# Soft-MoE attention kernel: four key chunks of 112, tokens transposed in 32x32 blocks on VectorE, slot sums in 16 array tiles

## The chip, the cores and the metric

The kernel runs on one core of a Trainium2 chip. A core has five engines that run side by side and wait for one another through semaphores: TensorE (PE in the profile, its weight loads PEld), VectorE (DVE), ScalarE (ACT), GpSimd (POOL) and SyncE (SP, which here only issues DMAs). Matrix products go from SBUF, the working memory, into PSUM, the memory of sums. The metric is the device time of one execution in microseconds, the median of several runs.

## What is computed

Eight batches of twelve heads, 448 tokens and 64 features per head. Attention uses a sigmoid in place of a softmax; its output, 3584 tokens of 768 features, goes through a soft mixture of experts with 32 slots (8 experts of 4).

```
scores = scale * q @ k.T - log(448);  attn = 1 / (1 + exp(-scores))
x = concat_heads(attn @ v)                          # (3584, 768)
logits = x @ phi                                    # (3584, 32)
d = softmax of logits over all tokens;  slot_input = d.T @ x      # (32, 768)
for e in range(8): slot_out[e] = relu(slot_input[e] @ w1[e]) @ w2[e]
c = softmax of logits over the 32 slots;  out = c @ slot_out      # (3584, 768)
```

All inputs are float32.

## The kernel before

**Attention.** The loop at L481 runs over 48 pairs of heads (six pairs `hp` to a batch `b`). A pair has the two heads' 64 features on the two halves of the 128 partitions. The 448 keys are cut into three chunks of 128 and a rest of 64. The rests of the two heads make one chunk of their own ("middle", step 0 of `qk_step` and `av_step`): a block-diagonal matrix of 128 x 128 with zeros beside each head's 64 keys, so that one product serves both heads. q and k are split into a high part rounded to fp32r and a low part, and a score is the sum of three fp32r products (high-high, high-low, low-high; L339 for the middle, L351 for the others, where the two heads' products lie on the two halves of the array's rows). ScalarE turns the scores into attention (`att`, L344 and L354). Attention times V (L375) is in plain fp32, two heads side by side in the array's columns; the middle chunk splits its attention and V too (L358, L144, L372). The sum `av` is copied to SBUF as `xT` (L381), 128 features by 448 tokens.

**Logits and slots.** `logits_job` (L183) adds a pair's part of the logits of a batch, four blocks of 112 tokens in four column groups of the array. `tr_job` (L193, L194) transposes `xT` on TensorE into `xtok`, token by feature. When a batch is complete, its softmax over tokens is carried along as a running maximum (`softmax_a` to `softmax_c`); `dt_job` transposes the weights on TensorE (L241), and `slot_job` forms weights times tokens (L251: eight products of 384 columns) and adds it to `acc`.

**Order.** All engines but POOL run in the order in which the program writes their instructions. For each pair the order is a string of tokens (L36 to L39): `Q1` to `Q3`, `V0` to `V3` are score and V steps, `P0` the next pair's middle scores, `L` and `T` the previous pair's logits and transposes, `k..`, `qp..`, `v..` the splits of the next pair, `l..` its loads. `EDGE`, `AFTER` and `THIRD` are the strings of a batch's first three pairs, in which the batch before is finished: its softmax in the first, its slot sums (`S0`, `S1`) in the second.

**Loads.** SP issues every DMA, in program order. Four tiles per pair (q with the middle keys, k, V, middle V) are loaded one or two pairs ahead, as the tiles come free. Beside them the expert weights are fetched in units of 384 KB (`load_unit`) into a ring: 55 tiles `wa` and two `kt` during attention, and twelve tiles `wb` whose space is that of the attention's tiles, and which can be loaded only as those are released, in order of address (the pools are opened as `ldq`, `ldr`, `sp`, `at`, `ldv`, `xp`). There are 128 units in all, so the other 59 follow as the experts free the ring.

**The rest.** `last_job` finishes the last batch; then the experts' first products (L517), the second ones (L630), and the output (`out_batch`), which writes 32 DMAs of 336 KB.

Of the kernel before, what the change touches and what calls it, by code (L numbers as in the profile page):

```python
# [26 lines left out]
N_A = 55  # L27
N_B = 12
QW = S + P
KW = 3 * P  # L30
# [5 lines left out]
ORDER = "n lq e mhV k00V k01 Q1 lw ml L T k10V Q2 k11 Q3 V0 qp0V qp1 lQ V1 V2 V3 P0 lv v0 v1 lr"  # L36
THIRD = "n lq e mhV k00V k01 sc Q1 ml L T k10V Q2 k11 lw Q3 V0 qp0V qp1 lQ V1 V2 V3 P0 v0 v1 lv lr"
EDGE = "e n k00V mhV k01 Q1 lq ml L sa T k10V Q2 k11 Q3 sb lw V0 qp0V qp1 lQ V1 V2 V3 P0 lv v0 sr v1 lr"
AFTER = "n mhV k00 eA Q1 dt lq ml k01 Q2 S0 k10V S1 k11 L lw T Q3 V0 qp0V qp1 lQ V1 V2 v0V V3 P0 v1 lr lv"  # L39
# [4 lines left out]
def soft_moe_attention(ctx: ExitStack, tc: tile.TileContext, qk, v, phi, w1, w2, cst, out):  # L44
# [6 lines left out]
    ldk = ctx.enter_context(tc.tile_pool(name="ldk", bufs=2))  # L51
# [8 lines left out]
    lt_all = cpool.tile([CH, NLT, P], F32, name="lt_all")  # L60
# [12 lines left out]
    def ring_tile(dt=F32):  # L73
        n = state["ring"]
        state["ring"] = n + 1
        n %= N_A + 2 + N_B
        if n < N_A:
            return wpa.tile([P, UNIT], dt, name=f"wa{n}")
        if n < N_A + 2:
            return ldk.tile([P, UNIT], dt, name="kt")  # L80
        return state["wpb"].tile([P, UNIT], dt, name=f"wb{n - N_A - 2}")

# [10 lines left out]
    lo, hi = slice(0, 64), slice(64, 128)  # L93
# [3 lines left out]
    lg_all = ps_lg.tile([P, 512], F32, name="lg")[:, 0:NLT * CH].rearrange("p (b t) -> p b t", b=NLT)  # L97

    with ExitStack() as actx:
        ldq = actx.enter_context(tc.tile_pool(name="ldq", bufs=1))  # L100
        ldr = actx.enter_context(tc.tile_pool(name="ldr", bufs=1))
        sp = actx.enter_context(tc.tile_pool(name="sp", bufs=1))
        at = [actx.enter_context(tc.tile_pool(name=f"at{i}", bufs=1)) for i in range(4)]
        ldv = actx.enter_context(tc.tile_pool(name="ldv", bufs=1))
# [5 lines left out]
        kts = {}  # L110
        qts = {}
        vts = {}
        vms = {}
        splits = {}
        xams = {}

        def load_k(p):
            kt = ldk.tile([P, UNIT], F32, name="kt")
            nc.sync.dma_start(kt[:, 0:KW], qk[p][:, QW:])
            kts[p] = kt  # L120

        def load_q(p):
            qt = ldq.tile([P, QW], F32, name="qt")
            nc.sync.dma_start(qt[:], qk[p][:, 0:QW])
            qts[p] = qt

        def load_v(p):
            vt = ldv.tile([P, NCH - 1, P], F32, name="vt")
            nc.sync.dma_start(vt[:], v[p][:, 1:, :])
            vts[p] = vt  # L130

        def load_vm(p):
            vm = ldr.tile([P, P], F32, name="vr")
            nc.sync.dma_start(vm[:], v[p][:, 0, :])
            vms[p] = vm

        def split_tiles(p):
            ks = [sp.tile([P, 2, P], F32R, name="ks0"), sp.tile([P, 2, KW], F32R, name="ks1", bufs=2)]
            qs = sp.tile([P, 2, S], F32R, name="qs")
            vm = sp.tile([P, 2, P], F32R, name="vm")  # L140
            splits[p] = (qs, ks, vm)

        def low_part(dst, src):
            nc.vector.tensor_tensor(out=dst[:, 1, :], in0=src, in1=dst[:, 0, :].bitcast(F32), op=ALU.subtract)  # L144

        def q_part(p, z, copy):
            qs = splits[p][0]
            if z == 0:
                copy(qs[:, 0, :], qts[p][:, 0:S])  # L149
            else:  # L150
                low_part(qs, qts[p][:, 0:S])

        def k_part(p, i, z, copy=nc.vector.tensor_copy):
            ks = splits[p][1][i]
            src = qts[p][:, S:] if i == 0 else kts[p][:, 0:KW]
            if z == 0:
                copy(ks[:, 0, :], src)
            else:
                nc.vector.tensor_tensor(out=ks[:, 1, :], in0=src, in1=ks[:, 0, :].bitcast(F32), op=ALU.subtract)  # L159

        def v_part(p, z, copy=nc.vector.tensor_copy):
            vm, src = splits[p][2], vms[p][:]
            if z == 0:
                copy(vm[:, 0, :], src)
            else:
                nc.vector.tensor_tensor(out=vm[:, 1, :], in0=src, in1=vm[:, 0, :].bitcast(F32), op=ALU.subtract)

        xtok = {}
        lgp = {}
        dts = {}  # L170
        av = {}
        xTs = {}
        atts = {}
        ams = {}

        def logits_job(p):
            b, hp = divmod(p, NPR)
            xT = xTs[p]
            if hp == 0:
                lgp[b] = lg_all[:, b % NLT, :]  # L180
                xtok[b] = xp.tile([CH, NCH, DM], F32, name="xtok")
            for j in reversed(range(NCH)):
                nc.tensor.matmul(  # L183
                    lgp[b][32 * j:32 * j + 32, :], phi_sb[:, hp, :], xT[:, j * CH:(j + 1) * CH],
                    start=(hp == 0), stop=(hp == NPR - 1),
                )

        def tr_job(p):
            b, hp = divmod(p, NPR)
            xT = xTs[p]  # L190
            pt = ps_ms.tile([P, NCH, P], F32, name="ms")
            for j in range(NCH):
                nc.tensor.transpose(out=pt[0:CH, j, :], in_=xT[:, j * CH:(j + 1) * CH], identity=ident)  # L193
            nc.scalar.copy(xtok[b][:, :, hp * P:(hp + 1) * P], pt[0:CH, :, :])  # L194

        def softmax_a(b):
            t1 = small.tile([P, 2, P], F32, name="t1")
            t2 = small.tile([P, 2, P], F32, name="t2")
            ls, zt = t2[:, 0, 0:CH], t1[:, 0, :]
            if b < NLT:  # L200
                nc.scalar.copy(ls, lgp[b])
            else:
                ls = lgp[b]
            if b == 0:
                nc.vector.tensor_reduce(out=mz[:, 0:1], in_=ls, axis=AX.X, op=ALU.max)
            else:
                m1 = small.tile([P, 2], F32, name="m1")
                nc.vector.tensor_reduce(out=m1[:, 0:1], in_=ls, axis=AX.X, op=ALU.max)
                nc.vector.tensor_copy(m1[:, 1:2], mz[:, 0:1])
                nc.vector.tensor_tensor(out=mz[:, 0:1], in0=m1[:, 0:1], in1=m1[:, 1:2], op=ALU.max)  # L210
                nc.vector.tensor_tensor(out=zt[:, CH:CH + 1], in0=m1[:, 1:2], in1=mz[:, 0:1], op=ALU.subtract)
            nc.vector.tensor_scalar(zt[:, 0:CH], ls, mz[:, 0:1], None, op0=ALU.subtract)
            dts[b] = (t1, t2)

        def softmax_b(b):
            t1, t2 = dts[b]
            zt, pe = t1[:, 0, :], t1[:, 1, :]
            n = CH if b == 0 else CH + 1
# [3 lines left out]
        def softmax_r(b):  # L222
            zt, pe = dts[b][0][:, 0, :], dts[b][0][:, 1, :]
            n = CH if b == 0 else CH + 1
# [3 lines left out]
        def softmax_c(b):  # L228
            pe = dts[b][0][:, 1, :]
            if b == 0:  # L230
                nc.vector.tensor_reduce(out=mz[:, 1:2], in_=pe[:, 0:CH], axis=AX.X, op=ALU.add)
            else:
                zb = small.tile([P, 1], F32, name="zb")
                nc.vector.tensor_reduce(out=zb[:], in_=pe[:, 0:CH], axis=AX.X, op=ALU.add)
                nc.vector.scalar_tensor_tensor(
                    out=mz[:, 1:2], in0=mz[:, 1:2], scalar=pe[:, CH:CH + 1], in1=zb[:], op0=ALU.mult, op1=ALU.add)

        def dt_job(b):
            t1, t2 = dts[b]
            pt = ps_ms.tile([P, NCH, P], F32, name="ms")  # L240
            nc.tensor.transpose(out=pt[0:CH, 1, :], in_=t1[:, 1, 0:CH], identity=ident)  # L241
            if b < NLT:
                nc.tensor.transpose(out=pt[0:CH, 0, :], in_=t2[:, 0, 0:CH], identity=ident)
            nc.vector.tensor_copy(t2[0:CH, 1, :], pt[0:CH, 1, :])
            if b < NLT:
                nc.scalar.copy(lt_all[:, b, :], pt[0:CH, 0, :])

        def slot_mm(b, hf, pt, dT):
            cs = slice(hf * HALF, (hf + 1) * HALF)
            for j in reversed(range(NCH)):  # L250
                nc.tensor.matmul(  # L251
                    pt[32 * j:32 * j + 32, 0:HALF], dT[:, 32 * j:32 * j + 32], xtok[b][:, j, cs],
                    start=True, stop=True)

        def slot_job(b, hf):
            pe, dT = dts[b][0][:, 1, :], dts[b][1][0:CH, 1, :]
            pt = ps_ms.tile([P, 512], F32, name="ms")
            cs = slice(hf * HALF, (hf + 1) * HALF)
            slot_mm(b, hf, pt, dT)
            if b == 0:  # L260
                nc.vector.tensor_copy(acc[:, cs], pt[:, 0:HALF])
            else:
# [431 lines left out]
```

## Time and profile before

| | us |
|---|---|
| median of 3 runs (466.55 to 466.9) | 466.64 |
| the profiled execution's own time | 465.93 |
| its span, first to last instruction | 464.1 |
| TensorE busy | 439.0 |
| VectorE busy | 267.4 |
| ScalarE busy | 235.5 |
| mean granted TensorE clock | 0.981 |

The span is what the profile explains; 1.83 us of the profiled execution's time lie outside it. A busy TensorE is not one at its peak: products are pipelined, and how far a step has moved is seen from the starts of one block and of the next, not from the busy time.

### The profile page before, as it was taken

What the parts mean: (1) busy time and instruction counts of PE and PEld (TensorE: products, weight loads), DVE (VectorE), ACT (ScalarE), POOL (GpSimd) and SP (SyncE); (2) the same over time, 40 slices, a digit from 0 to 9 for tenths busy, and PEclk for the clock granted to TensorE, in tenths of its full rate; (3) what the DMA queues carried; (4) which work ended last, traced back from release to release, by engine and by line L of the source; (5) the groups of instructions that cost most, each with busy time, mean ns of one, the idle gap of its engine ahead of it and who ended that gap; (6) DMA issues with size and microseconds to landing.
All of it is one profiled execution on the core that took longest, in us unless ns stands there. A gap on an engine that the chain in (4) does not pass through costs nothing.

```text
span 464.1 us, 8634 instructions
## 1 busy us (share of the span) xinstructions
PE 439.0 (95%) x3270; PEld 232.9 (50%) x3270; DVE 267.4 (58%) x735; ACT 235.5 (51%) x363; POOL 2.4 (1%) x12
## 2 busy tenths in 40 slices
PE   8999999999999999999999999999999999879870
PEld 5555555555545455454545555554545555334340
DVE  5656665576657565765666575666654544535280
ACT  4546554564646465555646455565547111544260
POOL 0000000000000000000000000000000100000000
PEclk9999999999999999999999999999999999998985
DMA  5666555665656566465755656633335999999998
GB/s 184 162 196 202 155 184 151 203 173 153 213 147 191 135 200 194 139 195 162 208 165 167 184 158 191 189 109 109 90 105 185 337 399 400 401 401 400 389 288 260
DMA packets 54089, 98.31 MB, mean 212 GB/s; under 512 B 5664, under 2 KB 31520, under 8 KB 54048
## 3 DMA queue, kind: packets, MB, share of 16 engines
q1 hardware_dynamic: 54048, 97.77, 65.6%
q8 instruction: 25, 0.41, 0.4%
q14 instruction: 16, 0.13, 0.1%
HBM read 86.74 MB, written 11.01 MB: 211 GB/s over the span
## 4 chain that ended last, share of the span: by engine, by line
PE 88%; DVE 4%; issue 2%; ACT 2%; DMA 1%; DVEq 0%; ACTq 0%
PE av L375 25%; PE sc L351 23%; PE av L372 8%; PE sc L339 8%; PE ms L193 6%; PE lg L183 3%; PE ph L517 3%; PE ms L251 2%; PE po L630 2%; PE ph L605 1%; PE pt L534 1%; PE pt L605 1%; PE av L392 1%; DMA out_dram<-wa 1%; DVE tmp L530 1%
## 5 line engine op out<-in xcount | busy, mean ns | idle before, releaser
L354 ACT ACTIVATE att<-sc,nbias 128x896 f32<-128x896 f32 x144 | 140.6, 1009 | 15.6 <-PE sc L351 10.1
L375 PE MATMUL av<-att,vt 128*64 128x448 f32 x576 | 118.8, 548 | 0.0
L351 PE MATMUL sc<-qs,ks 64*128 64x448 f32 x864 | 115.6, 387 | 0.3 <-ACT att L354 0.3
L344 ACT ACTIVATE att<-sc,nbias 128x448 f32<-128x448 f32 x48 | 30.5, 635 | 131.9 <-PE sc L339 131.9
L351 PEld LDWEIGHTS sc<-qs,ks 64*128 64x128 f32 x864 | 73.0, 184 | 28.1 <-issue 22.1
L381 DVE COPY att<-av 128x448 f32<-128x448 f32 x41 | 25.6, 625 | 72.9 <-PE av L375 72.9
L375 PEld LDWEIGHTS av<-att,vt 128*64 128x64 f32 x576 | 37.1, 136 | 59.2 <-issue 55.9
L358 DVE CAST ah<-att 128x448 fp32r<-128x448 f32 x48 | 18.9, 394 | 40.9 <-ACT att L344 40.9
L372 PE MATMUL av<-ah,vm 128*128 128x448 f32 x144 | 42.3, 401 | 0.0
L339 PE MATMUL sc<-qs,ks 128*128 128x448 f32 x144 | 41.9, 399 | 0.0
L339 PEld LDWEIGHTS sc<-qs,ks 128*128 128x128 f32 x144 | 23.6, 190 | 33.8 <-issue 27.5
L194 ACT COPY xtok<-ms 112x512 f32<-112x512 f32 x48 | 28.2, 587 | 10.3 <-PE ms L193 10.3
L372 PEld LDWEIGHTS av<-ah,vm 128*128 128x128 f32 x144 | 23.3, 188 | 15.9 <-DVE ks L159 7.8
L193 PE MATMUL ms<-csb,att 128*112 128x128 f32 x192 | 31.1, 285 | 0.0
L144 DVE TENSOR_TENSOR qs<-qt,qs 128x448 fp32r<-128x448 f32 x48 | 30.0, 626 | 1.6
L144 DVE TENSOR_TENSOR ah<-att,ah 128x448 fp32r<-128x448 f32 x48 | 29.7, 618 | 0.0
L159 DVE TENSOR_TENSOR ks<-kt,ks 128x384 fp32r<-128x384 f32 x48 | 26.8, 557 | 1.4
L149 DVE CAST qs<-qt 128x448 fp32r<-128x448 f32 x48 | 18.8, 392 | 8.9 <-PE sc L351 6.4
L193 PEld LDWEIGHTS ms<-csb,att 128*112 128x112 f32 x192 | 19.4, 133 | 8.2 <-issue 7.0
L183 PE MATMUL lg<-att,phit 128*32 128x112 f32 x384 | 19.0, 269 | 0.8 <-DVE att L381 0.8
L517 PE MATMUL ph<-wa,sT 128*32 128x256 f32 x330 | 19.6, 381 | 0.0
L609 DVE COPY wa<-pt 112x384 f32<-112x384 f32 x28 | 14.4, 554 | 5.1 <-PE pt L605 4.9
(142 smaller groups left out, 329.0 us busy)
## 6 DMA issues: line engine op xcount, KB each, us to landing
wa<-in_w_dram SPq DMA_DIRECT2D x110, 384.0 KB, 6.0
qt<-in_qk_dram SPq DMA_DIRECT2D x48, 288.0 KB, 2.8
out_dram<-wa SPq DMA_DIRECT2D x28, 336.0 KB, 4.9
kt<-in_qk_dram SPq DMA_DIRECT2D x48, 192.0 KB, 3.6
vt<-in_v_dram SPq DMA_DIRECT2D x48, 192.0 KB, 2.4
wb<-in_w_dram SPq DMA_DIRECT2D x14, 384.0 KB, 5.4
vr<-in_v_dram SPq DMA_DIRECT2D x48, 64.0 KB, 2.2
kt<-in_w_dram SPq DMA_DIRECT2D x4, 384.0 KB, 5.8
```

Source lines behind the costliest of these rows:

```text
L144: nc.vector.tensor_tensor(out=dst[:, 1, :], in0=src, in1=dst[:, 0, :].bitcast(F32), op=ALU.subtract)
L159: nc.vector.tensor_tensor(out=ks[:, 1, :], in0=src, in1=ks[:, 0, :].bitcast(F32), op=ALU.subtract)
L183: nc.tensor.matmul(lgp[b][32 * j:32 * j + 32, :], phi_sb[:, hp, :], xT[:, j * CH:(j + 1) * CH], start=(hp == 0), stop=(hp == NPR - 1),)
L193: nc.tensor.transpose(out=pt[0:CH, j, :], in_=xT[:, j * CH:(j + 1) * CH], identity=ident)
L194: nc.scalar.copy(xtok[b][:, :, hp * P:(hp + 1) * P], pt[0:CH, :, :])
L339: nc.tensor.matmul(sc[:, 0, 0:S], ks[0][:, z, :], qs[:, y, :], start=(z + y == 0), stop=(z == 1))
L344: nc.scalar.activation(am, sc[:, 0, 0:S], AF.Sigmoid, bias=nbias[:], scale=QSCALE)
L351: nc.tensor.matmul(sc[:, r.start // 64, 0:S], ks[1][r, z, (s - 1) * P:s * P], qs[r, y, :], start=(z + y == 0), stop=(z == 1))
L354: nc.scalar.activation(att[:], sc[:, :, 0:S], AF.Sigmoid, bias=nbias[:], scale=QSCALE)
L372: nc.tensor.matmul(av[p][:, 0:S], vm[:, z, :], att[:, y, :], start=(z + y == 0), stop=False)
L375: nc.tensor.matmul(av[p][64 * h:64 * h + 64, 0:S], vt[:, s - 1, 64 * h:64 * h + 64], att[:, h, :], start=False, stop=(s == 3))
L517: nc.tensor.matmul(ph[32 * j:32 * j + 32, uu, :], sT[:, 3 * kh + kc, :], utile[("w1", e, 2 * uu + j // 2, kh)][:, kc * 256:(kc + 1) * 256] ...
```

## The change

**Key chunks.** The keys are cut into four chunks of 112, all alike. The middle chunk, its splits and its zeros go. `split` makes the high and low parts of q and k with four VectorE instructions of 448 columns. q and k of a pair come in one DMA (448 KB), V in one (224 KB), the first into a single buffer, the second into two.

**Order.** The token strings go. One pair is: the previous pair's copy of `av`, all four score steps, the previous pair's logits, all four V steps, the splits of the next pair, the loads of the pair after that. The scores have three PSUM buffers in place of two.

**Tokens.** `tr_job` goes. VectorE transposes `xT` in blocks of 32 x 32 (`turn`), so a block of 32 tokens lies on each group of 32 partitions, with features in 32s. The order of the query tokens is permuted on the host so that the logits' blocks fit.

**Slots.** The softmax weights `pe` of a batch are transposed in the same way into `z`, and `spread` copies `z` with sixteen DMAs on SP so that every group of 32 partitions holds all of it (`dr`). `slot_mm` then makes 56 products of 192 columns in 16 tiles of 32 x 32 of the array (four row groups by four column groups). This is done in the second pair of the next batch, behind its V steps.

**Ring.** 56 tiles `wa`, none in `kt`, and 13 `wb`. `last_job` and the output follow the new layout: the last batch's weights are spread over the partitions by TensorE with the matrix `rep`, and the tokens of a batch go out in two groups, two times 128 and two times 96.

```diff
-N_A = 55
-N_B = 12
+N_A = 56
+N_B = 13
-        ps_sc = actx.enter_context(tc.tile_pool(name="ps_sc", bufs=2, space=PSUM))
+        ps_sc = actx.enter_context(tc.tile_pool(name="ps_sc", bufs=3, space=PSUM))
-        ps_ms = actx.enter_context(tc.tile_pool(name="ps_ms", bufs=2, space=PSUM))
...
+        def split(p, i, z, copy=nc.vector.tensor_copy):
             if z == 0:
+                splits[p, i] = sp.tile([P, 2, S], F32R, name=("qs", "ks")[i])
+            dst, src = splits[p, i], qkts[p][:, i * S:(i + 1) * S]
+            if z == 0:
+                copy(dst[:, 0, :], src)
             else:
+                nc.vector.tensor_tensor(out=dst[:, 1, :], in0=src, in1=dst[:, 0, :].bitcast(F32), op=ALU.subtract)
...
+        def qk_step(p, c):
+            qs, ks = splits[p, 0], splits[p, 1]
+            sc = ps_sc.tile([P, 2, 512], F32, name="sc")
+            for z, y in ((0, 0), (0, 1), (1, 0)):
+                for h, r in enumerate(heads):
+                    nc.tensor.matmul(
+                        sc[0:CH, h, 0:S], ks[r, z, c * CH:(c + 1) * CH], qs[r, y, :], start=(z + y == 0), stop=(z == 1))
+            att = at.tile([CH, 2, S], F32, name=f"att{c}")
+            nc.scalar.activation(att[:], sc[0:CH, :, 0:S], AF.Sigmoid, bias=nbias[0:CH, :], scale=QSCALE)
+            atts[p, c] = att
+
+        def av_step(p, c):
+            if c == 0:
+                av[p] = ps_av.tile([P, 512], F32, name="av")
+            for h, r in enumerate(heads):
+                nc.tensor.matmul(
+                    av[p][r, 0:S], vts[p][:, c, r], atts[p, c][:, h, :], start=(c == 0), stop=(c == NCH - 1))
+
+        def evac(p, copy=nc.vector.tensor_copy):
+            xTs[p] = xp.tile([P, S], F32, name="xT", bufs=2)
+            copy(xTs[p][:], av[p][:, 0:S])
+
+        def turn(p):
+            b, hp = divmod(p, NPR)
+            if hp == 0:
+                ys[b] = xp.tile([P, NPR, S], F32, name="y")
+            nc.vector.transpose(ys[b][:, hp, :], xTs[p][:])
...
+        def spread(b):
+            z = small.tile([P, P], F32, name="z")
+            nc.vector.transpose(z[:], dts[b][:, 1, 0:P])
+            dr = xp.tile([P, NBK, P], F32, name="dr")
+            for a in range(4):
+                for j in range(4):
+                    n = P if j < 3 else S - 3 * P
+                    nc.sync.dma_start(dr[32 * a:32 * a + 32, j, 0:n], z[32 * j:32 * j + 32, 0:n])
+            drs[b] = dr
+
+        def slot_mm(b):
+            sl = [ps_sc.tile([P, 2, 512], F32, name="sc") for _ in range(2)]
+            y = ys[b]
+            for c in range(NBK):
+                for a in range(4):
+                    for j in range(4 if c < 2 else 3):
+                        k = NBK * j + c
+                        nc.tensor.matmul(
+                            sl[a // 2][32 * j:32 * j + 32, a % 2, 0:NPR * BLK],
+                            drs[b][32 * a:32 * a + 32, j, c * BLK:(c + 1) * BLK],
+                            y[32 * a:32 * a + 32, :, k * BLK:(k + 1) * BLK],
+                            start=(c == 0), stop=(c == (3 if j < 3 else 1)))
+            return sl
...
+        for p in range(NP):
             b, hp = divmod(p, NPR)
             nxt = p + 1 < NP
+            while state["next"] < min(N_A, (p + 1) * N_A // 40):
+                load_unit()
+            if p > 0:
+                evac(p - 1)
+            for c in range(NCH):
+                qk_step(p, c)
+            if p > 0:
+                logits_job(p - 1)
+                if hp == 2 and b > 0:
+                    turn(p - 2)
+                if not (hp == 1 and b > 0):
+                    turn(p - 1)
+            if hp == 0 and b > 0:
                 softmax_a(b - 1)
                 softmax_b(b - 1)
+            for c in range(NCH):
+                av_step(p, c)
+            if nxt:
+                split(p + 1, 0, 0)
+                split(p + 1, 0, 1)
+                split(p + 1, 1, 0)
+                split(p + 1, 1, 1)
+            load_qk(p + 2)
+            load_v(p + 2)
+            if hp == 0 and b > 0:
                 softmax_r(b - 1)
                 softmax_c(b - 1)
+                spread(b - 1)
+            if hp == 1 and b > 0:
+                slot_job(b - 1)
```

The pools are now opened as `ldq` (q and k, one buffer), `ldv` (V, two buffers), `sp`, `at`, `xp`. `slot_job` adds the four results of `slot_mm` to `acc` with two VectorE instructions of 384 columns.

More of the change, by code (lines that the diff above doesn't have):

```diff
@@ L137, in split_tiles @@
[L137 to L147, printed above, removed]
+        qkts, vts, splits, av, xTs, ys, dts, drs = {}, {}, {}, {}, {}, {}, {}, {}
@@ L153, in k_part @@
[L153 to L166, printed above, removed]
@@ L176, in logits_job @@
         def logits_job(p):
             b, hp = divmod(p, NPR)
[L178 to L194, printed above, removed]
@@ L196, in softmax_a @@
-        def softmax_a(b):
[L197 to L203, printed above, removed]
+            for j in reversed(range(4)):
+                n = P if j < 3 else S - 3 * P
+                nc.tensor.matmul(
+                    lg_of(b)[32 * j:32 * j + 32, 0:n], phi_sb[:, hp, :], xTs[p][:, j * P:j * P + n],
+                    start=(hp == 0), stop=(hp == NPR - 1))
@@ L248, in slot_mm @@
[L248 to L262, printed above, removed]
-                nc.vector.scalar_tensor_tensor(
-                    out=acc[:, cs], in0=acc[:, cs], scalar=pe[:, CH:CH + 1], in1=pt[:, 0:HALF],
-                    op0=ALU.mult, op1=ALU.add)
+                    out=mz[:, 1:2], in0=mz[:, 1:2], scalar=pe[:, P:P + 1], in1=zb[:], op0=ALU.mult, op1=ALU.add)
@@ new lines, in acc_of, with slot_job @@
+        def acc_of(g):
+            return acc[:, g * HALF:(g + 1) * HALF].rearrange("p (a n) -> p a n", a=2)
+        def slot_job(b):
+            sl = slot_mm(b)
+            for g in range(2):
+                part = sl[g][:, :, 0:NPR * BLK]
+                if b == 0:
+                    nc.vector.tensor_copy(acc_of(g), part)
+                else:
+                    nc.vector.scalar_tensor_tensor(
+                        out=acc_of(g), in0=acc_of(g), scalar=dts[b][:, 1, P:P + 1], in1=part,
+                        op0=ALU.mult, op1=ALU.add)
@@ L481, in soft_moe_attention @@
-        for p in range(NP):
-            b, hp = divmod(p, NPR)
-            for tok in (ORDER if b == 0 or hp > 2 else (EDGE, AFTER, THIRD)[hp]).split():
-                run(tok, p)
-        new_xt(NP)
+                spread(b - 1)
+            if hp == 1 and b > 0:
+                slot_job(b - 1)
+        dmx = small.tile([1, 1], F32, name="dmx")
+        nc.scalar.activation(dmx[:], atts[NP - 1, 3][0:1, 0, 0:1], AF.Exp)
         evac(NP - 1)
         logits_job(NP - 1)
-        tr_job(NP - 1)
+        turn(NP - 1)
@@ L499, in soft_moe_attention @@
         elif e < 6:
-            h = small.tile([P, 256], F32, name=("phit", "t1", "t2")[e - 3])[:]
+            h = small.tile([P, 256], F32, name=("phit", "t1", "z")[e - 3])[:]
         else:
```

391 lines of the change are left out of this document (117 added, 274 removed).

## The prediction

> **What bounds the kernel now.** I read the page first, for the engine without gaps and for the chain of work that ended last.
>
> ```profile
> span 464.1 us, 8634 instructions
> ...
> PE 439.0 (95%) x3270; PEld 232.9 (50%) x3270; DVE 267.4 (58%) x735; ACT 235.5 (51%) x363; POOL 2.4 (1%) x12
> ...
> PEclk9999999999999999999999999999999999998985
> DMA  5666555665656566465755656633335999999998
> ...
> PE 88%; DVE 4%; issue 2%; ACT 2%; DMA 1%; DVEq 0%; ACTq 0%
> ```
>
> TensorE is 88% of the chain, and until slice 30 of 40 the DMA engines are half idle; from there on they are full. So there are two stages, attention bound by TensorE and experts by DMA. Next the timeline of TensorE for one pair in the middle (start, duration).
>
> ```profile
> 199.82 0.40 PE L183 MATMUL lg<-att,phit 128*32 128x112 f32 x8
> 200.15 0.65 PE L193 MATMUL ms<-csb,att 128*112 128x128 f32 x4
> 200.73 1.49 PE L351 MATMUL sc<-qs,ks 64*128 64x448 f32 x12
> 202.15 0.88 PE L372 MATMUL av<-ah,vm 128*128 128x448 f32 x3
> 202.96 2.48 PE L375 MATMUL av<-att,vt 128*64 128x448 f32 x12
> 205.36 0.86 PE L339 MATMUL sc<-qs,ks 128*128 128x448 f32 x3
> 206.16 0.88 PE L351 MATMUL sc<-qs,ks 64*128 64x448 f32 x6
> 206.96 0.40 PE L183 MATMUL lg<-att,phit 128*32 128x112 f32 x8
> ```
>
> The starts, not the durations, are the cost: logits 0.33, transposes 0.58, two score chunks 1.42, middle V 0.81, three V chunks 2.40, middle scores 0.80, one score chunk 0.80: 7.14 us, without a gap. One chunk (three steps of two products side by side) costs 0.80, a second in the same block only 0.62. So a step is 0.207, and entering a block costs 0.18.
>
> The end of this stage and the DMA stage, from the timelines of SP and TensorE and from the windows (PE, PEld, DVE, ACT, POOL busy, clock, DMA share, GB/s):
>
> ```profile
> 354.47 6.12 SPq L90 DMA_DIRECT2D wb<-in_w_dram  x8
> 358.12 2.48 PE L375 MATMUL av<-att,vt 128*64 128x448 f32 x12
> 355.00:373.00 18.00, 17.13 (x200) 10.09 (x198) 7.80 (x26) 6.42 (x11) 2.18 (x8) 1.00 0.96 338
> 373.00:441.00 68.00, 59.88 (x656) 28.48 (x648) 29.29 (x92) 23.20 (x70) 0.00 (x0) 0.97 1.04 399
> ```
>
> The last V products end at 360.6, yet the DMA engines have been full since the first `wb` unit at 354.5: the rest of the run is paced from there, 109.6 us to the end of the span, and 103.5 us after the last V product.
>
> **The change, part by part.** *Scores.* Twelve steps in one block: 0.18 + 12 x 0.207 = 2.66. A fourth chunk waits until ScalarE has emptied the first of three buffers:
>
> ```profile
> 207.07 1.01 ACT L354 ACTIVATE att<-sc,nbias 128x896 f32<-128x896 f32 x1
> ```
>
> ```profile
> 7.00 1.02 ACT att L354
> ...
> 8.06 0.89 PE sc L351 x6
> ```
>
> ScalarE starts 0.91 after a chunk's block begins (206.16 to 207.07), takes 1.01, and TensorE resumes 0.05 later (the first pair, 8.02 to 8.06): 1.97, just when TensorE arrives. Refilling the array costs about 0.1: I take 0.12. Bounds: 0 and 0.3.
>
> *V.* The fp32 weight loads of a chunk come every 0.375 us, twice per chunk:
>
> ```profile
> 203.76 0.14 PEld L375 LDWEIGHTS av<-att,vt 128*64 128x64 f32 x2 [0.23 <-issue]
> ...
> 204.51 0.14 PEld L375 LDWEIGHTS av<-att,vt 128*64 128x64 f32 x2 [0.23 <-issue]
> ```
>
> So four chunks cost 2.40 + 0.75 = 3.15. The last attention chunk is there at about 0.91 + 4 x 1.01 = 4.95 after the pair's start, and the fourth V chunk begins at 2.78 + 0.36 + 2.40 = 5.5: no wait.
>
> *Logits* go from 112 to 128 columns: 0.33 x 128/112, 0.36 with rounding. *Transposes* leave TensorE.
>
> A pair is 2.66 + 0.12 + 0.36 + 3.15 = **6.29**, 0.85 less than now. Over 48 pairs that is 40.8 us.
>
> *Beside TensorE.* VectorE has per pair the copy of `av`, a block transpose and four splits.
>
> ```profile
> L144 DVE TENSOR_TENSOR qs<-qt,qs 128x448 fp32r<-128x448 f32 x48 | 30.0, 626 | 1.6
> ...
> L149 DVE CAST qs<-qt 128x448 fp32r<-128x448 f32 x48 | 18.8, 392 | 8.9 <-PE sc L351 6.4
> ...
> qt<-in_qk_dram SPq DMA_DIRECT2D x48, 288.0 KB, 2.8
> ```
>
> Splits take 2 x (0.39 + 0.63) = 2.0, and can begin when the scores have released `qs`, at 2.85; they end at 4.9 and are wanted at 6.29. No row shows a block transpose: 0.39 if it is a cast, 0.63 if it is like the subtraction; 0.6 taken, and 1.2 would still fit before 2.85. The single q/k buffer is reloaded at 4.95. 288 KB land in 2.8; 448 KB at 338 GB/s about 0.5 later, 8.3, and the next split wants it at 6.29 + 2.85 = 9.1. If that cover of 0.8 and the splits' 1.4 were used up, each 0.1 us would cost 4.8 us over the loop.
>
> *Between batches* (seven times). Now, 360.6 - 5.2 (the first scores) - 48 x 7.14 leaves 12.7, 1.8 each. Of the new path, these show the parts:
>
> ```profile
> 184.99 0.27 DVE L208 TENSOR_REDUCE m<-t 128x1 f32<-128x112 f32 x1
> ...
> 185.81 0.36 DVE L157 CAST ks<-kt 128x384 fp32r<-128x384 f32 x1
> ...
> 187.98 0.86 DVE L225 RECIPROCAL t<-t 128x113 f32<-128x113 f32 x1
> ```
>
> ```profile
> 2.60 0.43 SPq L387 DMA_DIRECT2D csb<-in_cst_dram  x1
> 3.08 0.43 SPq L388 DMA_DIRECT2D phit<-in_phi_dram  x1
> 3.55 0.43 SPq L119 DMA_DIRECT2D kt<-in_qk_dram  x1
> 5.05 0.33 SPq L124 DMA_DIRECT2D qt<-in_qk_dram  x1
> ```
>
> ```profile
> vr<-in_v_dram SPq DMA_DIRECT2D x48, 64.0 KB, 2.2
> ```
>
> Count from the start of a batch's first pair. Logits of the batch before end at 3.3. VectorE: `softmax_a` 0.82 (184.99 to 185.81) and, in half the batches, a block transpose of 128 columns (0.3): 4.5. The next pair's splits are written ahead of the rest: 6.5. Its third score step wants the last part only at 6.29 + 0.5, so no wait. The reciprocal 0.9, its product and two small sums 0.7 (each like the reduction's 0.27 or less), the transpose into `z` 0.3: **8.4**. Only then can SP issue `spread`'s sixteen DMAs. Three issues in a row stand 0.475 apart (2.60 to 3.55, of 128, 96 and 192 KB), whatever their size; a lone one takes 0.33. No row shows one of 16 KB. I take the row: the last is issued at 8.4 + 15 x 0.47 = 15.5. 64 KB land after 2.2; I take 2.0 for 16 KB: **17.5**. The second pair's V steps end at 12.6. So TensorE waits 4.9 us in `slot_mm`. Behind it in TensorE's order is all the next pair; behind the sixteen issues on SP stand the weight units, and q/k of the fourth pair, issued at 17 instead of 11 and landed by 21.5, which the splits want at 22: hidden by the wait alone.
>
> After the last landing come the products of the remaining groups:
>
> ```profile
> 192.00 1.50 PE L251 MATMUL ms<-xtok,t 112*32 112x384 f32 x16
> 193.31 0.38 PE L183 MATMUL lg<-att,phit 128*32 128x112 f32 x8
> ```
>
> Eight products of 384 columns in four column groups take 1.31. Forty-one of 192 columns, if four row groups run at once as two do in the scores: four rounds of half that length, 1.3. If row groups take turns: 5. I take 1.3. The Trainium skill ("TensorE: Matmul & The Clock Gate", Part 3) gives 16 tiles a measured speed-up of 10.6, an estimate of 0.65 us more per batch, 4.5 in all; no row here shows four row groups. Then the next pair waits for VectorE to empty two buffers: 0.3. Together 6.5.
>
> *The clock.* Such a wait has its own price; windows of the tail, where TensorE waits for weights:
>
> ```profile
> 394.94:398.35 3.41, 2.10 (x24) 0.96 (x22) 1.47 (x5) 0.95 (x5) 0.00 (x0) 1.00 1.03 401
> 415.42:418.83 3.41, 0.99 (x3) 0.37 (x3) 1.11 (x2) 1.10 (x3) 0.00 (x0) 1.00 1.03 402
> 418.83:422.25 3.42, 3.42 (x14) 1.67 (x15) 1.12 (x2) 0.96 (x2) 0.00 (x0) 0.51 1.03 399
> ```
>
> A window of 3.41 us with TensorE busy 0.99 is followed by one at half clock (0.51); after one with 2.10 the page's clock row stays at 9. However such windows fall over 4.9 us, one of them holds at least 2.45 of it and is left with less than 0.99. On average some 2.8 us of the slow window then lie behind the wait and half of them is lost: 1.4. A boundary is **7.9**; seven are 55.3, against 12.7 now.
>
> *The tail.* The ring's space is that of the attention's tiles in order of address: `wb` 0 fits into q/k, `wb` 1 lies over both V buffers, so it waits for the last V product, and SP holds all behind it. 71 units are then still to come, as now at 354.5, so the DMA stage starts with the end of the loop: 109.6 after it in place of 103.5, **6.1 more**. Bounds: 0 and 7. The changes in `last_job` and the output lie under it, 1 us either way.
>
> **Sum.** -40.8 + (55.3 - 12.7) - 0.4 (no logits in the first pair) + 6.1 = +7.5 on the profiled execution's 465.9 (span 464.1 and 1.8 around it): 473.4. The median of the runs stands 0.7 above that execution: **474**.
>
> **The rivals.** *The clock stays.* The wait isn't quite idle: a product of the first group can run each time one of the sixteen DMAs lands, every 0.47 us for some 0.3 us. If these sixteenths of the array keep the clock, as the window with 2.10 did, 1.4 x 7 = 9.8 goes: 464.2, **faster than before** by 0.5%. It decides on whether the 0.99 of the table is time or work done, which no row tells. The Trainium skill (same page, Part 1) throttles after an idle window; by that rule, taken literally, such a wait wouldn't count. I give it 0.26.
>
> *Small DMAs are quick.* With 0.38 between issues (0.33 and the gap of 0.05) and 1.6 to land, `dr` is there at 15.7 and the wait is 3.1: 12.6 us less in all, and the clock drops in some batches only: 452 to 460. For it: a quarter of the rows per DMA. Against: the issue rows, equal over sizes. 0.14.
>
> *The row groups take turns.* 5 in place of 1.3: 26 us more, 500. The score products' two row groups do run at once, so 0.06.
>
> **How the numbers follow.** The forecast has 0.48, the rivals 0.26, 0.14 and 0.06; 0.06 remain for a loop held by VectorE or by the q/k buffer. Faster: 0.14, 0.20 of the 0.26, 0.04 of the forecast (a shorter wait): 0.38. Within 0.2%, which is about what a measurement of this kernel can tell from no change: 0.05 + 0.04 = 0.09. Slower 0.53. The range takes the forecast's own 467 to 481 (issue spacing, tail, 0.1 us per pair) and goes down over the rival with the full clock to 457: 457 to 481, with a tenth left out on each side.
>
> **What the profile would show.** A pair of 6.3 us from one block of scores to the next (6.15 without the fourth chunk's wait). At each batch, in the second pair, TensorE idle before `slot_mm`'s products, released by the `dr` DMA; sixteen SP issues 0.47 apart. A clock row with 8s spread over the loop; if it stays 9 the first rival holds. All `wb` units but the first issued behind the last V product. Wrong at the root would be a pair over 6.8, or TensorE waiting for VectorE's splits in every pair.

## The result and the profile after

The changed kernel takes 505.51 us (median of four runs, 503.27 to 507.61), the kernel before 466.60 (four runs, 465.34 to 466.90): a ratio of 1.084, 95% interval 1.077 to 1.091. The forecast was 474.0, with 457 to 481 as its range: the sign was right, and the loss of 39 us is five times the one foreseen. The changed kernel's four runs lie in two pairs some 4 us apart, so a gain or loss of a few us against it is known to about 2 us only. The execution profiled below took 507.6.

The page of the changed kernel, in the lines that answer to those shown of before:

```profile
span 505.8 us, 9886 instructions
...
PE 459.2 (91%) x4030; PEld 229.3 (45%) x4030; DVE 225.4 (45%) x512; ACT 216.6 (43%) x300; POOL 2.5 (0%) x12
...
PEclk9999979989997999699979995999799898989865
DMA  5665266525643565346345624532132699999996
...
PE 67%; DVE 12%; SPq 9%; issue 3%; DMA 2%; ACT 1%; ACTq 0%; DVEq 0%
PE sc L137 24%; PE av L147 21%; SPq L213 9%; PE sc L223 7%; PE ph L395 3%; PE lg L164 3%; DMA dr<-z 2%; PE po L502 2%; PE ph L480 2%; PE pt L480 1%; DVE t L193 1%; PE pt L412 1%; DVE ks L128 1%; DVE qs L128 1%; DVE xT L152 1%
```

TensorE was 88% of the chain that ended last and is 67%. What has grown is VectorE (from 4% to 12%), and what has come in are the sixteen issues of `spread` on SP (L213, 9%) and their landings (`dr<-z`, 2%). The clock row, before an unbroken line of 9s through the loop, has seven dips there, one for each batch but the last; the DMA row has holes at the same places.

TensorE's timeline over one batch boundary (start, duration, matmul records; two records are one fp32 product):

```profile
188.57 2.89 PE L137 MATMUL sc<-qs,ks 64*112 64x448 f32 x24
...
194.91 2.83 PE L137 MATMUL sc<-qs,ks 64*112 64x448 f32 x24
197.67 0.43 PE L164 MATMUL lg<-xT,phit 128*32 128x64 f32 x8
198.03 3.23 PE L147 MATMUL av<-att,vt 112*64 112x448 f32 x16
201.19 2.53 PE L223 MATMUL sc<-y,dr 32*32 32x192 f32 x16
203.94 1.03 PE L223 MATMUL sc<-y,dr 32*32 32x192 f32 x4 [0.22 <-DMA dr<-z]
...
209.22 2.70 PE L223 MATMUL sc<-y,dr 32*32 32x192 f32 x82 [0.16 <-DMA dr<-z]
211.85 4.25 PE L137 MATMUL sc<-qs,ks 64*112 64x448 f32 x24
...
219.54 2.89 PE L137 MATMUL sc<-qs,ks 64*112 64x448 f32 x24
```

The pair is what it was meant to be: 6.34 from one block of scores to the next (188.57 to 194.91). But from 201.19 to 211.85 the queue stands at the slot products, 82 of whose 112 records come behind the last landing, and the scores after them take 4.25 in place of 2.8. SP's timeline at the same place has the reason:

```profile
197.02 10.81 SPq L213 DMA_DIRECT2D dr<-z  x16
207.88 0.57 SPq L85 DMA_DIRECT2D wa<-in_w_dram  x1
208.56 0.36 SPq L112 DMA_DIRECT2D qkt<-in_qk_dram  x1
```

The sixteen issues take 10.81 us of SP's time. The means over all seven boundaries, counted from the first scores of the pair before the wait (188.57 above):

| us, mean of seven | forecast | changed kernel |
|---|---|---|
| first issue of `spread` | 8.4 | 8.31 |
| last issue | 15.5 | 18.17 (17.5 to 18.8) |
| last landing (last issue + 1.8) | 17.5 | 20.0 |
| slot products begin | 12.6 | 12.61 |
| next scores begin | 19.1 | 22.60 |
| those scores, start to start of the logits behind them, over 2.83 | 1.4 (the clock) | 0.97 |
| boundary: 22.60 - 12.61 + 0.97 | 7.9 | 10.96 |

So a boundary costs 3.06 more than forecast, seven cost 21.4. The other large difference is the tail. SP's timeline at its start, the waits of SP (engine, line, what it waited for: us, times, longest), and windows of it (PE, PEld, DVE, ACT, POOL busy, clock, DMA share, GB/s):

```profile
378.99 23.47 SPq L85 DMA_DIRECT2D wb<-in_w_dram  x13
403.08 55.09 SPq L85 DMA_DIRECT2D wa<-in_w_dram  x56
```

```profile
SPq L85 <- DVE qs L290: 6.8, 1, 6.8
...
SPq L85 <- PE av L147: 6.6, 1, 6.6
```

```profile
386.00:392.00 6.00, 5.26 (x148) 3.65 (x148) 3.18 (x11) 1.13 (x5) 0.62 (x2) 1.00 0.25 70
392.00:398.00 6.00, 4.23 (x42) 2.83 (x46) 2.31 (x10) 0.00 (x0) 1.68 (x6) 0.85 0.32 93
398.00:404.00 6.00, 6.00 (x92) 3.19 (x88) 2.69 (x10) 0.64 (x3) 0.00 (x0) 0.87 0.95 326
```

The last V product ends at 386.0, but the DMA engines are a quarter to a third busy for another 12 us. From 386.0 to the end of the span are 119.8; 109.6 was forecast. The forecast's span was 473.4 - 1.8 = 471.6. With 21.4 for the boundaries, 10.2 for the tail and 48 x 0.05 = 2.4 for the pairs it is 505.6, and 505.8 was measured: these three terms are the whole error.

### The profile page after: what moved, and what is told of

It is laid out like the page before. It is cut to its first block, busy times and chain, and to the rows that moved or that the text cites. A ratio compares the mean times of both kernels' runs of the same rounds, so it can differ in the third digit from the quotient of the medians.

```text
span 505.8 us, 9886 instructions
## 1 busy us (share of the span) xinstructions
PE 459.2 (91%) x4030; PEld 229.3 (45%) x4030; DVE 225.4 (45%) x512; ACT 216.6 (43%) x300; POOL 2.5 (0%) x12
## 4 chain that ended last, share of the span: by engine, by line
PE 67%; DVE 12%; SPq 9%; issue 3%; DMA 2%; ACT 1%; ACTq 0%; DVEq 0%
PE sc L137 24%; PE av L147 21%; SPq L213 9%; PE sc L223 7%; PE ph L395 3%; PE lg L164 3%; DMA dr<-z 2%; PE po L502 2%; PE ph L480 2%; PE pt L480 1%; DVE t L193 1%; PE pt L412 1%; DVE ks L128 1%; DVE qs L128 1%; DVE xT L152 1%
## 5 line engine op out<-in xcount | busy, mean ns | idle before, releaser
L140 ACT ACTIVATE att<-sc,nbias 112x896 f32<-112x896 f32 x192 | 178.5, 1008 | 197.2 <-PE sc L137 196.6
L147 PE MATMUL av<-att,vt 112*64 112x448 f32 x768 | 154.9, 545 | 0.0
L137 PE MATMUL sc<-qs,ks 64*112 64x448 f32 x1152 | 146.0, 395 | 0.0
L137 PEld LDWEIGHTS sc<-qs,ks 64*112 64x112 f32 x1152 | 100.6, 184 | 59.5 <-issue 28.4
L147 PEld LDWEIGHTS av<-att,vt 112*64 112x64 f32 x768 | 50.8, 136 | 76.5 <-issue 73.3
L223 PE MATMUL sc<-y,dr 32*32 32x192 f32 x896 | 63.5, 465 | 9.1 <-DMA dr<-z 6.2
L152 DVE COPY xT<-av 128x448 f32<-128x448 f32 x48 | 29.6, 617 | 49.2 <-PE av L147 49.2
L126 DVE CAST qs<-qkt 128x448 fp32r<-128x448 f32 x48 | 18.7, 389 | 66.1 <-PE sc L137 35.5
L128 DVE TENSOR_TENSOR qs<-qkt,qs 128x448 fp32r<-128x448 f32 x48 | 30.0, 625 | 1.6
L128 DVE TENSOR_TENSOR ks<-qkt,ks 128x448 fp32r<-128x448 f32 x48 | 30.0, 625 | 1.6
L158 DVE STREAM_TRANSPOSE y<-xT 128x448 f32<-128x448 f32 x48 | 30.1, 637 | 1.2
L164 PE MATMUL lg<-xT,phit 128*32 128x128 f32 (+1 forms) x384 | 20.5, 271 | 0.7 <-DVE xT L152 0.7
```

Source lines behind the costliest of these rows:

```text
L126: copy(dst[:, 0, :], src)
L137: nc.tensor.matmul(sc[0:CH, h, 0:S], ks[r, z, c * CH:(c + 1) * CH], qs[r, y, :], start=(z + y == 0), stop=(z == 1))
L140: nc.scalar.activation(att[:], sc[0:CH, :, 0:S], AF.Sigmoid, bias=nbias[0:CH, :], scale=QSCALE)
L147: nc.tensor.matmul(av[p][r, 0:S], vts[p][:, c, r], atts[p, c][:, h, :], start=(c == 0), stop=(c == NCH - 1))
L152: copy(xTs[p][:], av[p][:, 0:S])
L158: nc.vector.transpose(ys[b][:, hp, :], xTs[p][:])
```

## The experiments

Theory after the result: the issues of `spread` are dear on SP, TensorE and the loads behind them wait for that, and a scratch tile of the last batch holds the ring of `wb`. Rivals: the lowered clock is the main cost; or a wait elsewhere (the transposes on VectorE, the splits) is.

**The scratch tile of the last batch elsewhere.**

```diff
-            total = sp.tile([P, DM], F32, name="qs")
+            total = at.tile([P, DM], F32, name="att3")
```

> One edit: the scratch tile of the last batch's sums lies over the fourth attention tile instead of over the split q. Theory (expert weights held up): after the last V product the second weight unit waits until the split q's space is released, some 9 us later, and SP holds all others behind it. With the edit the units go out when the last V product has ended: the stretch from the last V product to the end shrinks from 119.9 us to about 110, the time from 505.5 to about 496. Rival (the longer last batch itself, or the output in groups of 256 and 192 rows, makes the tail longer): no change, 505.

499.75 us, ratio 1.071 (1.067 to 1.075). The `wb` units, from SP's timeline:

```profile
376.57 18.72 SPq L85 DMA_DIRECT2D wb<-in_w_dram  x13
```

18.7 us for them instead of 23.5; from the last V product (384.2) to the end (496.6) are 112.4, 7.4 less. The gain in time is 5.8, a little short of that. The tile was the cause of most of the tail's error. What is left of it, 2.8, goes with a wait of SP for the tile at its new place, though no run shows that this wait is all of it (a row of SP's waits):

```profile
SPq L85 <- DVE att L290: 4.0, 1, 4.0
```

**The array kept at work in the wait.**

```diff
+            pw = ps_sc.tile([P, 2, 512], F32, name="sc")
+            for _ in range(18):
+                nc.tensor.matmul(pw[:, 0, 0:256], ident, csb[:, 0:256], start=True, stop=True)
             sl = slot_mm(b)
```

> One edit: 18 full-array products of 256 columns (7.7 us of dummy work) stand ahead of the slot products, in the time in which TensorE waits for the copies of the weights. Theory (the low clock costs): the granted clock stays at 1.00 through the loop, the products behind the last landing take 1.6 us instead of 2.6 and the next pair's scores 2.8 instead of 4.1, 2.5 to 3 us per batch, seven times: about 487. Rival (the clock is of no weight, the 56 products in 16 tiles are slow by themselves): within 3 us of 505.

500.63 us, ratio 1.073 (1.070 to 1.076): 5 less where 18 were expected and the rival allowed 3, so neither holds as worded. TensorE's timeline at the same boundary:

```profile
200.00 8.04 PE L236 MATMUL sc<-csb 128*128 128x256 f32 x36
207.97 2.19 PE L223 MATMUL sc<-y,dr 32*32 32x192 f32 x112
210.09 2.91 PE L137 MATMUL sc<-qs,ks 64*112 64x448 f32 x24
```

The clock was 1.00 through the whole loop, and the boundary still takes 10.09: 7.97 of extra products and 2.12 of slot products, from start to start. Nothing waits for a landing any more. But the extra products end 20.58 after the first scores, the last copy lands at 20.05 (means of the seven), and all 56 slot products stand behind them where 41 did. So the added work itself sets this boundary, and part of what the clock gave back is hidden in it. The run shows that full clock alone doesn't repair the boundary; what the clock costs it doesn't show.

**The spread on TensorE, no DMA at all.** Four products of `rep` with `z` in the middle of the second pair's V steps, two copies out of them on VectorE and ScalarE.

```diff
-                    nc.sync.dma_start(dr[32 * a:32 * a + 32, j, 0:n], z[32 * j:32 * j + 32, 0:n])
+                nc.tensor.matmul(pd[j // 2][:, j % 2, 0:P], rep[r, :], zs[b][r, :], start=True, stop=True)
...
+            nc.vector.tensor_copy(dr[:, 0:2, :], pd[0][:, :, 0:P])
+            nc.scalar.copy(dr[:, 2, :], pd[1][:, 0, 0:P])
+            nc.scalar.copy(dr[:, 3, 0:64], pd[1][:, 1, 0:64])
```

> The sixteen DMAs per batch go; the weights are spread over the partitions by four TensorE products in the midst of the V steps and copied from PSUM by VectorE and ScalarE. Theory (the wait for the copies, with the clock that it brings down, is the whole cost of a batch's end): 11 us per batch become about 3 (0.6 for the four products and the change of shape, 2.2 for the slot products at full clock, 0.3): 7 x 8 = 56 us less, about 449. Rival (the slot products in 16 tiles or VectorE's added work hold the loop as well): 470 to 490.

449.55 us, ratio 0.964 (0.960 to 0.967), as expected. TensorE's timeline:

```profile
176.81 0.50 PE L215 MATMUL sc<-z,csb 32*128 32x128 f32 x8
177.24 1.72 PE L147 MATMUL av<-att,vt 112*64 112x448 f32 x8
178.89 2.20 PE L232 MATMUL sc<-y,dr 32*32 32x192 f32 x112
181.02 2.91 PE L137 MATMUL sc<-qs,ks 64*112 64x448 f32 x24
```

A boundary is now 0.43 + 2.13 = 2.6, and the clock stays at 1.00 through the loop, without any added work. The rest of the change (pairs, transposes, slots in sixteen tiles) stands in it untouched: the whole loss of the loop hangs on the sixteen DMAs.

**Both repairs.** The last two edits together:

> Both edits, the spreading by TensorE and the scratch tile over the fourth attention tile. If the two causes add: 449 - 10 = about 440, below the kernel before (466.6). If the weight units are held by something else once the loop is shorter: about 449.

443.13 us, ratio 0.949 (0.947 to 0.951): 6.4 less than with the spreading alone, where the tile alone had gained 5.8, so they add up. The 440 expected took the tail's whole error of 10.2 for the gain. A version with `total` in the space of `y` and the V buffers at the end of the ring:

> Spreading by TensorE; the last batch's scratch tile lies over the block-transposed tokens (free when the slot products are done), and the V buffers are allotted last, so that the first weight units' space is that of q, k and their splits, which come free 3.5 us before the last V product. Theory (the end is paced by DMA from the time when the weight units can go out): the stretch behind the last V product goes from 114.0 us to about 111, the time from 443 to about 440. Rival (it is paced by the experts' first products, which wait for the last batch): 443 to 445.

442.22 us, ratio 0.946 (0.942 to 0.950), with 113.0 behind the last V product. The difference to 443.13 lies inside the intervals, and 113.0 lies between the two forecasts' figures: moving the tile and the buffers gains nothing that these runs can tell. Both versions are faster than the kernel before and the changed one. The 3.4 us still missing to 109.6 go with another such wait, for `total` lies in the ring's space again; that it is all of the 3.4 isn't shown. The waits of SP:

```profile
SPq L85 <- DVE y L299: 5.0, 1, 5.0
```

**What makes an issue dear: the source, or its rows.** In the first of two kernels the sixteen DMAs read a constant from HBM, same shape, same target; in the second they stay inside SBUF but take all 128 rows, 128 bytes each.

```diff
-                    nc.sync.dma_start(dr[32 * a:32 * a + 32, j, 0:n], z[32 * j:32 * j + 32, 0:n])
+                    nc.sync.dma_start(dr[32 * a:32 * a + 32, j, 0:n], cst[32 * j:32 * j + 32, 0:n])
```

```diff
+                    nc.sync.dma_start(dr[:, j, 32 * a:32 * a + 32], z[:, 32 * a:32 * a + 32])
```

> The sixteen DMAs of a batch keep their targets, sizes and place, but read a constant in HBM in place of the weights' tile in SBUF, so the slot sums leave out the weights. The issues of the change stood 0.63 us apart, where those of the kernel before stood 0.47. If the source in SBUF makes an issue dear: 0.47 apart here, and with the start 1 us earlier (nothing to wait for on VectorE) the last copy is there some 4 us sooner in each batch: about 475. If 32 rows to a DMA make it dear: 0.63 apart as before, only the earlier start gains: about 497.

> Sixteen DMAs again from the weights' tile in SBUF, but each of 128 rows by 32 columns (128 bytes a row) straight across, with the same 16 KB; nothing is spread over the partitions, so the slot sums are those of other weights. If the source in SBUF makes an issue dear: 0.63 apart. If 32 rows do: 0.47 apart. Above 0.63 would be the short rows' own price.

From HBM: 480.28 us, ratio 1.029 (1.022 to 1.036). From SBUF with 128 rows: 498.36, ratio 1.068 (1.062 to 1.073). The instructions of tile `dr` on SP (duration in ns, least, median, most), first of the changed kernel, then of the HBM one, then of the one with 128 rows:

```profile
L213 SPq DMA_DIRECT2D dr<-z x112: 507/588/1498, 51.5 to 355.3; - x112
```

```profile
L213 SPq DMA_DIRECT2D dr<-in_cst_dram x112: 311/419/1646, 51.6 to 328.9; - x112
```

```profile
L213 SPq DMA_DIRECT2D dr<-z x112: 465/599/1657, 51.5 to 347.6; - x112
```

One of these issues takes 0.42 from HBM and 0.59 or 0.60 from SBUF, whatever its rows; from start to start the medians are 0.46, 0.63 and 0.64. So the row length is out: with the same target, the source makes these issues dear. A source in SBUF doesn't do so everywhere: the first five output DMAs of the changed kernel, from SBUF to HBM, were issued in 0.39, though the 27 behind them took 1.38 (medians). No run varies the target of the sixteen, so whether it counts too stays open.

```profile
L483 SPq DMA_DIRECT2D out_dram<-wb x5: 340/388/951, 461.8 to 465.8; - x5
```

With HBM the last issue stands at 14.96 in the mean (forecast 15.5), the next scores at 18.94 (19.1) and the boundary is 18.94 - 12.61 + 0.77 = 7.1, where 7.9 was forecast. The first issue needn't wait for `z` there and stands at 7.52, 0.8 earlier than in the changed kernel; with that put back, an estimate of 7.9. With the source of the row that the forecast used, its sum holds. The last issue came 3.2 sooner and not 4, so the time is 480 and not 475.

The kernel with 128 rows gains 7 us on the changed one with issues that are no cheaper. Its copies fill one column block of `dr` after the other, in the order in which the products need them, so at most 10 of the 112 records stand behind the last landing instead of 82, and the next scores begin at 20.75 instead of 22.60. The order of the copies is a lever of its own.

**The slot products a pair later.** `slot_job` after the third pair instead of the second, three buffers of `xT`, one ring unit less, and the block transposes that must wait for `y` a pair later too.

```diff
...
-            if hp == 1 and b > 0:
+            if hp == 2 and b > 0:
                 slot_job(b - 1)
```

> The sixteen DMAs stay as the change has them, but the slot products stand one pair later (behind the third pair's V steps), so the copies have 6.3 us more; a third buffer for the transposed-to-be tokens is paid with one tile of the ring. Theory (SP's queue is the second way in which the sixteen issues cost: the fourth pair's q and k stand behind them): the wait in front of the slot products goes, but the third pair's splits and then the fourth pair's scores wait for q and k, 5 to 6 us per batch: 485 to 495. Rival (only the slot products' wait costs, and SP's queue has room): as with the spreading by TensorE, 450 to 457.

495.49 us, ratio 1.061 (1.056 to 1.067). TensorE's, VectorE's and SP's timelines:

```profile
204.11 3.18 PE L223 MATMUL sc<-y,dr 32*32 32x192 f32 x112
210.46 4.21 PE L137 MATMUL sc<-qs,ks 64*112 64x448 f32 x24 [3.17 <-DVE ks L126]
```

```profile
208.95 0.39 DVE L126 CAST qs<-qkt 128x448 fp32r<-128x448 f32 x1 [10.43 <-DMA qkt<-in_qk_dram]
```

```profile
193.63 10.79 SPq L213 DMA_DIRECT2D dr<-z  x16
...
205.23 0.36 SPq L112 DMA_DIRECT2D qkt<-in_qk_dram  x1
```

The slot products wait for nothing now. But the q/k load stands behind the sixteen issues and goes out at 205.23, the splits wait 10.43 for it, and TensorE for them. The forecast had named that queue and called it hidden by the wait alone; with the wait gone it comes to light. Moving the consumer doesn't help while the issues sit in the queue of the loads.

**What the clock goes by.** Two kernels put small work into the wait: one full-array product of 128 columns ahead of each of the sixteen products that wait for a landing, or eight 32x32 products there.

```diff
...
+                        if c == 0 and pw is not None:
+                            nc.tensor.matmul(pw[:, 0, 0:P], ident, ident, start=True, stop=True)
```

```diff
...
+                        for i in range(8 if c == 0 and b < B - 1 else 0):
+                            a2, j2 = i % 3, (i // 3 + 3 * j) % 4
+                            nc.tensor.matmul(
+                                to[a2][32 * j2:32 * j2 + 32, :], csb[32 * a2:32 * a2 + 32, 0:32],
+                                y[32 * a2:32 * a2 + 32, :, 0:BLK], start=True, stop=True)
...
```

> The changed kernel with one extra full-array product of 128 columns (two passes, about 0.36 us, result unused) ahead of each of the sixteen slot products of the first group. They lie in the stretch in which TensorE waits for the sixteen issues, 0.63 us apart, so they put no work behind the last landing and keep the array at work for about 5.7 us of the wait. What differs from the changed kernel is then the clock alone. Theory: in the changed kernel the half clock costs about 2 us per batch, 1.0 in the products behind the last landing (2.6 instead of 1.6) and 1.0 in the scores behind them; with the clock at 1.00 through the loop the next scores start about 21.6 us after the first scores of the pair before the wait, where they start at 22.6 now, and the time is 505.5 - 14 = 491.5 us. Rival: what the eighteen products ahead of the wait saved, 0.7 us per batch, is all that the clock costs: 500 us.

> The changed kernel with eight extra 32x32 products of 192 columns (a constant's block times y, results unused) ahead of each of the sixteen slot products of the first group, in three of the four row groups, so that no product of another size stands between; av is copied before them and not after. By the 56 products of the last batch in 2.19 us with sixteen tiles, eight take about 0.42 us with twelve tiles: less than the 0.63 between two issues, so nothing is added behind the last landing. TensorE is busy in the wait as before, but with over half of the array. Theory (the clock goes by the work done, and its half costs about 2 us per batch): clock 1.00 through the loop, the next scores 21.6 us after the first scores of the pair before the wait where they stand 22.6 after now, scores in 2.9 instead of 3.8: 491.5 us. Rival 1: the clock costs only the 0.7 us per batch that the eighteen products saved: 500 us. Rival 2: even this work is too little, or it takes longer than the issues: clock halves, 505 us or more.

The first took 592.66 us, ratio 1.268 (1.265 to 1.272), a clear miss. Its timeline of TensorE and a window over the same stretch:

```profile
180.34 0.49 PE L225 MATMUL sc<-csb 128*128 128x128 f32 x2
180.76 0.51 PE L226 MATMUL sc<-y,dr 32*32 32x192 f32 x2
...
187.66 0.80 PE L225 MATMUL sc<-csb 128*128 128x128 f32 x2
188.39 0.84 PE L226 MATMUL sc<-y,dr 32*32 32x192 f32 x2
```

```profile
182.60:203.10 20.50, 20.50 (x134) 10.33 (x135) 1.58 (x3) 0.02 (x1) 0.00 (x0) 0.50 0.30 95
```

A full-array and a 32x32 product in turn don't overlap: each takes 0.42 from start to start at full clock, 0.73 at half. So the sixteen pairs of products outlast the landings by far (the next scores begin at 35.5, in the mean, instead of 22.60), and the run can't tell what the clock costs. But the clock stays at 0.50 for 20.5 us in which TensorE is never idle: it doesn't go by busy time.

The second took 507.53, ratio 1.089 (1.085 to 1.094), no better than the changed kernel. The clock was 1.00 through the loop, the scores behind the wait took 2.82, so 0.98 came back there; but the last issue stood at 18.86 instead of 18.17 and the next scores at 23.30 instead of 22.60. From the last landing to the next scores were 1.89 instead of 2.67, so another 0.8 came back there: together 1.8 per batch, near the 2 of the theory. The time doesn't show it, since the last landing came 1.5 later, at 21.41 instead of 19.93. Why SP issued later, and why some copies took longer to land, isn't settled. In the two kernels that kept the clock by added work the boundary is 10.1 and 10.7 in place of 10.96, and with the copies gone the clock stayed up by itself: the lowered clock follows from the wait, costs some 2 us of the 11, and is not the main cost.

## Why the prediction was wrong

*Right.* The pair: 6.29 forecast, 6.34 measured. The block transpose, put between 0.39 and 0.63 and taken at 0.6, is 637 ns in the page's groups:

```profile
L158 DVE STREAM_TRANSPOSE y<-xT 128x448 f32<-128x448 f32 x48 | 30.1, 637 | 1.2
```

The start of `spread` (8.4 against 8.31), the landing (2.0 against 1.8), the four row groups at once, the waits before `slot_mm` and the dips of the clock came as described. The 56 slot products take 2.19 at full clock, so 41 take 41/56 x 2.19 = 1.60; 1.3 was forecast. The Trainium skill ("TensorE: Matmul & The Clock Gate", Part 3) gives sixteen tiles a speed-up of 10.6, by which an estimate would have been 1.95; 1.60 lies between the two.

*Wrong: "Three issues in a row stand 0.475 apart ..., whatever their size ... I take the row."* This is the step that failed. The row was of loads from HBM, the sixteen DMAs copy from SBUF to SBUF, and such an issue takes 0.59 where one of the same shape from HBM takes 0.42 (median against median in the two kernels). With some that take up to 1.5, the fifteen steps from first to last issue took 18.17 - 8.31 = 9.9 instead of 7.1: 2.8 more per boundary. The rest of its 3.06 are small terms: the start 0.1 and the landing 0.2 earlier, the products behind it 2.6 instead of 1.6, the scores 0.4 cheaper. The step also mistook what the row's sameness showed: it held over sizes, not over sources. And the range left 7 us above the forecast for the issues, the tail and the pairs together, where the boundaries alone were off by 21.4.

*Wrong: the tail's "Bounds: 0 and 7".* The forecast followed the ring over the attention's tiles only as far as the V buffers. The next unit lies over the split q, whose space `last_job` takes again for `total` (L290), so SP waited for VectorE there another 6.8. The tail was 10.2 longer than forecast, and 7.4 came back when the tile moved; the other 2.8 are open.

*The first rival* asked whether the 0.99 of the table was time or work. TensorE was busy 2.70 of 3.41 in the window of the changed kernel behind which the clock fell, against 2.10 in the window of before behind which it stayed:

```profile
201.61:205.02 3.41, 2.70 (x16) 0.66 (x10) 0.00 (x0) 0.00 (x0) 0.00 (x0) 1.00 0.11 27
205.02:208.44 3.42, 2.25 (x9) 0.86 (x10) 0.00 (x0) 0.00 (x0) 0.00 (x0) 0.50 0.08 19
208.44:211.85 3.41, 3.25 (x85) 1.70 (x84) 0.00 (x0) 0.00 (x0) 0.00 (x0) 0.50 0.81 273
211.85:215.26 3.41, 3.41 (x22) 2.84 (x20) 2.75 (x5) 1.73 (x2) 0.00 (x0) 0.50 0.48 162
```

So busy time doesn't decide it, and the rival fell. The kernel with eight extra products bears this out, in windows of the same wait:

```profile
207.20:210.61 3.41, 1.75 (x98) 1.22 (x92) 0.00 (x0) 0.00 (x0) 0.00 (x0) 1.00 0.27 41
210.61:214.02 3.41, 3.41 (x89) 2.46 (x74) 2.22 (x4) 1.37 (x2) 0.00 (x0) 1.00 0.96 355
```

TensorE was busy 1.75 there, with 98 records in place of 16, and the clock stayed. That it goes by the work done in the array fits all these windows; no run isolates it. The Trainium skill (same page, Part 1) speaks of an idle window; taken literally this doesn't agree with the trace, since the clock fell with TensorE 79% busy, and stayed down in the experiment with TensorE never idle. The half clock also lasted more than the one window forecast: three of them here and at one more boundary, two at the other five. Behind the landing it shows as 1.0 in the products (2.6 against 1.60) and 0.97 in the scores, 2.0 where 1.4 was forecast. *Small DMAs are quick* fell with the issue's 0.59; *row groups take turns* with the 2.19.

## What to carry to other kernels

Price a DMA issue by a row with the same kind of source and target, and count all the issues of a step as time of the queue that the loads share: the chain of sixteen small copies between partitions was dearer here than four products on TensorE. When a stage's buffers lie over another's, follow the order of the ring through every tile that takes the space again, scratch of the last batch included. Small products in a long wait held the clock only where they came densely (98 records in 3.41 us, not 16), and filling the wait gained 5 us at most here, where removing it gained 56.

## What was not expected of the hardware

The issue of a DMA of 16 KB (8 KB in four of the sixteen) took 0.59 us from SBUF to SBUF and 0.42 from HBM, with the same rows and target. Full-array and 32x32 products in turn cost 0.42 each at full clock, where the 56 products of 32x32 alone take 2.19 together (0.04 per product). The clock stood at 0.50 for 20.5 us with TensorE busy throughout, and at 1.00 behind a window with TensorE busy 1.75 of 3.41.
